# An attention-then-feed-forward kernel on one core: float32 loads for three head pairs, fills written ahead of loads, another order of loads, and a head pair moved behind the first feed-forward units

## The chip, the cores and the metric

The kernel runs on 1 core of one Trainium2 chip. The metric is the device time of one execution in microseconds; lower is better. Runs of one kernel agree within 1%, mostly within 0.5%. The profile is of one execution; its span (first to last instruction) is about 2 us shorter than the timed figure.

## The reference

```python
# attention: B, H, S, D = 8, 8, 576, 64, float32
scores = q @ k^T / 8 + bias[bucket(|i - j|)]      # T5 bias: a 32-entry table for each head
attn = softmax(scores);  x = attn @ v              # -> x: (B*S, H*D) = (4608, 512)
# bilinear feed-forward
a = x @ w_a;  b = x @ w_b                          # 512 -> 1536
out = (a * b) @ w_out                              # 1536 -> 512
```

## The kernel before

The heads are taken in pairs: 8 batches of 4 pairs, 32 in all, so pair 4 is the first of batch 1. 576 positions are 512 ("main") and 64 ("tail"). A pair takes scores on TensorE, the exponential on ScalarE, a multiply by the exponential of the bias on VectorE (only near the diagonal), and the product with V on TensorE. A column of ones beside V makes the sum of the softmax. The feed-forward work is cut into units (`ff_a`, `ff_b`, `ff_o`), which are put between the steps of the pairs from stage 4 on, so that TensorE is never without work. Stage s means the steps issued around pair s.

All loads before the first stage, in the order of the program (float32 to bf16 is cast on the way in GpSimd's queue):

```python
for p in range(2):                                    # pairs 0 and 1 in float32
    for h in range(2):
        load_h(nc.sync, q, q32[:, p, :, h, :], 0, 2 * p + h)
        load_h(nc.scalar, k, k32[:, p, :, h, :], 0, 2 * p + h)
# ... fills, bias table computed ...
nc.sync.dma_start(out=tab.ap(), in_=tab_sb[0:H, :])   # the table goes to HBM
load_w(nc.sync, 0)                                    # and comes back as W, one band for each pair
# ... Wt, the band of the tails, two transfers ...
load_w(nc.sync, 1)

load_tails(0)                    # GpSimd's queue from here on: tails of batches 0 and 1
load_t(q, qn, 0, 4, 8)           # pairs 2 and 3
load_t(k, kn, 0, 4, 8)
load_v(0)
load_pad(v, vt, 0)               # V's tails of batches 0 and 1
load_t(q, qn, 1, 0, 8)           # batch 1
load_t(k, kn, 1, 0, 8)
load_w_in(0)
load_w_in(1)
load_v(1)                        # V of batch 1, into vm[1]
load_w_in(2)
```

The first four pairs run without units. Stage 0 ends so:

```python
for s in range(4):
    ex(s, 0)
    if s > 0:
        mul(s - 1, 3)                                 # last bias multiply of the pair before
        mul_tail(s - 1)
    # ... transposes of the next pair, scores, exponentials, product with V ...
    mul(s, 2)
    # ...
    if s == 0:
        for i in range(2):
            nc.vector.memset(att_sb[i][:, 1088:1152], 0.0)
        nc.vector.memset(vm[1][:, :, :, Dh:Dh + 1], 1.0)      # ones beside V, second buffer
```

Stage 4 (pair 4) has its scores ahead of the first unit `U`; the number of units of each stage is in `quotas`:

```python
quotas = {4: 5, 5: 7, 6: 7, 7: 7, 8: 7}               # 9 from stage 9 on
steps += [mul(3, 3), mul_tail(3), t_x(2, FF), c_x(2),
          t_q(4, TR), c_q(4, ACT), t_k(4, FF), c_k(4),
          A(0, 1, 2), N(0), qk1(4, 0), ex(4, 0), A(3, 4), N(3),
          qk1(4, 1), ex(4, 1), t_x(3, TR), c_x(3),
          t_q(5, FF), qk1(4, 2), ex(4, 2), c_q(5),
          qk1(4, 3), ex(4, 3), U, mul(4, 0), ...]     # lambdas left out here
```

The program order is kept on every engine. The framework adds a semaphore wait wherever an instruction touches a buffer that an earlier one in the program writes.

The softmax here doesn't subtract the row's maximum and nothing guards it: scores larger than these inputs give would overflow.

## Time and profile before

| | before |
|---|---|
| time, median of 4 (3 were known for the prediction: 452.51) | 452.88 us (452.20 to 453.74) |
| span of the profiled run | 450.3 us |
| TensorE busy | 414.0 us (92%) |
| VectorE, longest wait | 25.6 us, once |

In all views PE is TensorE (PEld its weight loads), DVE VectorE, ACT ScalarE, POOL GpSimd and SP SyncE; L328 is line 328 of the kernel. The page first: busy time of the engines, then tenths of TensorE's busy time, of its granted clock and of the 16 DMA engines in 40 equal slices of 11.26 us.

```profile
span 450.3 us, 8335 instructions
...
PE 414.0 (92%) x3350; PEld 204.5 (45%) x3350; DVE 196.7 (44%) x488; ACT 241.8 (54%) x340; POOL 112.3 (25%) x142
...
PE   7311899999999999999999999999999999999995
...
PEclk9755999999999999999999999999999999999999
DMA  9999999969990999099909990941021002002004
```

The 92% is an average of two kernels: slices 2 to 4 hold little TensorE work (three tenths to one tenth), nearly all others are full. The same in figures, by the windows view (packets overlap, so its DMA share can pass 1):

```profile
core 0: us, PE busy (x) PEld busy (x) DVE busy (x) ACT busy (x) POOL busy (x), PEclk, DMA share, GB/s
11.00:22.00 11.00, 4.41 (x31) 2.02 (x29) 2.47 (x9) 6.43 (x8) 10.19 (x13) 0.72 1.80 159
22.00:33.00 11.00, 2.13 (x23) 1.65 (x24) 0.00 (x0) 0.00 (x0) 8.69 (x11) 0.50 3.25 141
33.00:44.00 11.00, 0.76 (x13) 0.76 (x13) 1.89 (x9) 0.46 (x2) 7.25 (x10) 0.50 1.75 183
...
112.00:450.00 338.00, 333.78 (x2551) 159.52 (x2548) 143.03 (x330) 184.70 (x265) 44.75 (x54) 1.00 0.72 77
```

Between 22 and 33 us neither VectorE nor ScalarE runs anything. The list of waits of the first 90 us (engine and line, what released it, us in all, times, longest) says who is to blame:

```profile
DVE at L328 <- DMA vm<-in_v_dram: 25.6, 1, 25.6
ACT att L347 <- PE qktt L340: 23.4, 2, 23.2
...
PE qktt L340 <- DVE QT L229: 15.6, 1, 15.6
...
PE av L370 <- DMA vt<-in_v_dram: 6.2, 1, 6.2
```

Linked together: ScalarE (L347) waits for TensorE (L340), TensorE for VectorE (L229), VectorE for the load of V. But line 328 is the bias multiply, and it reads no V. VectorE's timeline (start, us, then what ran, and in brackets the idle time before it) shows the real one:

```profile
15.93 0.55 DVE L328 TENSOR_TENSOR at<-at,W 128x768 bf16<-128x768 bf16 x1
16.43 0.13 DVE L566 MEMSET att<- 128x32 uint32 x2
42.11 0.45 DVE L328 TENSOR_TENSOR at<-at,W 128x512 bf16<-128x512 bf16 x1 [25.56 <-DMA vm<-in_v_dram]
42.23 0.09 DVE L567 MEMSET vm<- 128x32 bf16 x1
42.48 0.25 DVE L354 TENSOR_TENSOR att<-att,Wt 128x192 bf16<-128x192 bf16 x1
```

In the program the memset of line 567 stands directly after the two of line 566, ahead of the multiply. It writes the ones into `vm[1]`, and `load_v(1)`, which writes the same buffer, stands far above it in the program. So it waits for that load. The last part landed at 41.98 us; the record of the semaphore wait in VectorE's queue carries line 567 and stands at 42.01 us. The multiply's record begins at 42.11 us, ahead of the memset's at 42.23, though it stands behind it in the program; so the idle time was booked to the multiply.

### The profile page before, as it was taken

The page shows a single profiled execution, that of the slowest core. Times are in us where ns is not written, and L with a number is a line of the kernel's source. Part 1 is how long each engine was busy: PE and PEld are TensorE (multiplying, and loading weights), DVE is VectorE, ACT ScalarE, POOL GpSimd, SP SyncE. Part 2 cuts the span into 40 slices and gives each one's busy share as a digit, 9 for nine tenths or more (in the row PEclk, how much of TensorE's full clock was granted, in tenths as well). Part 3 has the DMA queues.
Part 4 walks back from the last instruction along what each step waited for, and adds up shares of the span by engine and source line. Part 5 has one row for each costly group of instructions (what it writes and reads, how often), then busy time and mean ns, then how long its engine had stood idle before and what let it go on. Part 6 is the DMA issues. An engine that isn't in the chain of part 4 may idle for free.

```text
span 450.3 us, 8335 instructions
## 1 busy us (share of the span) xinstructions
PE 414.0 (92%) x3350; PEld 204.5 (45%) x3350; DVE 196.7 (44%) x488; ACT 241.8 (54%) x340; POOL 112.3 (25%) x142
## 2 busy tenths in 40 slices
PE   7311899999999999999999999999999999999995
PEld 3111555455444444454445444544454454444442
DVE  5102867554455345534553455345534550330330
ACT  3501866565666566656665666566656642323321
POOL 8885750608300910092009100300000000000000
PEclk9755999999999999999999999999999999999999
DMA  9999999969990999099909990941021002002004
GB/s 148 156 148 184 182 155 166 92 40 130 166 108 13 112 185 110 13 109 192 117 13 115 185 104 15 143 120 38 13 84 38 15 13 96 0 1 93 0 1 93
DMA packets 173895, 41.74 MB, mean 93 GB/s; under 512 B 160408, under 2 KB 169248, under 8 KB 173856
## 3 DMA queue, kind: packets, MB, share of 16 engines
q0 software_dynamic: 116336, 18.36, 65.9%
q1 hardware_dynamic: 55264, 22.22, 27.8%
q10 hardware_dynamic: 2256, 0.62, 0.7%
q8 instruction: 26, 0.43, 0.4%
q14 instruction: 13, 0.11, 0.1%
HBM read 38.83 MB, written 9.45 MB: 107 GB/s over the span
## 4 chain that ended last, share of the span: by engine, by line
PE 88%; DMA 5%; POOL 3%; DVE 1%; ACT 1%; issue 1%; DVEq 0%; ACTq 0%; POOLq 0%
PE pb L444 22%; PE pa L434 21%; PE po L454 21%; PE av L379 9%; PE qk L309 7%; DMA vm<-in_v_dram 4%; PE av L370 2%; PE qkt L334 2%; DMA kn<-in_k_dram 2%; PE qkt L337 1%; POOL vm L131 1%; POOL kn L122 1%; POOL qn L122 1%; PE trx L412 1%; DVE XG L388 1%
## 5 line engine op out<-in xcount | busy, mean ns | idle before, releaser
L320 ACT ACTIVATE at<-qk 128x1024 bf16<-128x1024 f32 x128 | 126.3, 1024 | 29.3 <-PE qk L309 28.8
L447 DVE TENSOR_TENSOR g<-pb,ha 128x512 bf16<-128x512 f32 x108 | 74.7, 691 | 123.7 <-PE pb L444 104.9
L434 PE MATMUL pa<-xn,wa 128*128 128x512 bf16 x432 | 111.0, 379 | 0.0
L444 PE MATMUL pb<-xn,wb 128*128 128x512 bf16 x432 | 110.9, 379 | 0.0
L438 ACT ACTIVATE ha<-pa 128x512 f32<-128x512 f32 x108 | 64.6, 598 | 70.8 <-PE pa L434 70.7
L454 PE MATMUL po<-wo,g 128*128 128x512 bf16 x432 | 102.5, 379 | 0.0
L328 DVE TENSOR_TENSOR at<-at,W 128x512 bf16<-128x512 bf16 (+1 forms) x128 | 60.4, 483 | 39.0 <-DMA vm<-in_v_dram 25.6
L444 PEld LDWEIGHTS <-wb 128*128 128x128 bf16 x432 | 38.7, 97 | 52.5 <-issue 17.2
L434 PEld LDWEIGHTS <-wa 128*128 128x128 bf16 x432 | 38.9, 98 | 50.4 <-issue 11.0
L131 POOL DMA_DIRECT2D vm<-in_v_dram x32 | 28.2, 909 | 126.3 <-PE av L379 125.0
L454 PEld LDWEIGHTS <-g 128*128 128x128 bf16 x432 | 38.4, 98 | 45.9 <-issue 7.6
L458 ACT ACTIVATE ob<-po 128x512 f32<-128x512 f32 x36 | 21.5, 597 | 68.3 <-PE po L454 68.3
L379 PE MATMUL av<-vm,at 128*128 128x65 bf16 x1024 | 48.1, 196 | 0.0
L379 PEld LDWEIGHTS <-at 128*128 128x128 bf16 x1024 | 43.4, 99 | 6.6
L370 PE MATMUL av<-vt,att 128*128 128x130 bf16 x160 | 35.5, 222 | 6.2 <-DMA vt<-in_v_dram 6.2
L387 DVE RECIPROCAL rc<-av 128x6 f32<-128x6 f32 x64 | 12.0, 188 | 54.2 <-PE av L379 54.2
L348 ACT ACTIVATE att<-qkt 128x1024 bf16<-128x1024 f32 x32 | 32.7, 1022 | 0.0
L122 POOL DMA_DIRECT2D qn<-in_q_dram x32 | 27.9, 911 | 17.9 <-PE trq L263 17.6
L388 DVE TENSOR_TENSOR XG<-av,rc 128x384 bf16<-128x384 f32 x64 | 31.4, 491 | 2.2
L122 POOL DMA_DIRECT2D kn<-in_k_dram x32 | 27.9, 910 | 8.4 <-DMA vt<-in_v_dram 5.1
L309 PE MATMUL qk<-QTb,KTb 64*128 64x512 bf16 x192 | 29.1, 381 | 0.0
L347 ACT ACTIVATE att<-qktt 128x64 bf16<-128x64 f32 x32 | 7.2, 225 | 29.0 <-PE qktt L340 28.8
(96 smaller groups left out, 211.8 us busy)
## 6 DMA issues: line engine op xcount, KB each, us to landing
out_dram<-ob SPq DMA_DIRECT2D x32, 256.0 KB, 3.5
vm<-in_v_dram POOLq DMA_DIRECT2D x32, 128.0 KB, 6.1
qn<-in_q_dram POOLq DMA_DIRECT2D x28, 128.0 KB, 9.2
kn<-in_k_dram POOLq DMA_DIRECT2D x28, 128.0 KB, 11.8
wa<-in_moe_w_a_dram POOLq DMA_DIRECT2D x6, 256.0 KB, 8.5
wb<-in_moe_w_b_dram POOLq DMA_DIRECT2D x6, 256.0 KB, 8.5
wo<-in_moe_w_out_dram POOLq DMA_DIRECT2D x1, 1536.0 KB, 16.9
out_dram<-ob SPq DMA_DIRECT2D x8, 128.0 KB, 2.3
```

Of the source, the lines that this page charges most:

```text
L122: nc.gpsimd.dma_start(out=dst[b % 2][:, :].rearrange("p (t h d) -> p t h d", h=H, t=NM)[:, t, h0:h1, :], in_=src[b, h0:h1, 128 * t:128 * t ...
L309: nc.tensor.matmul(out=ps[:, hh, :], lhsT=kT_(p, t)[r, :], rhs=qT[r, :, :], start=True, stop=True)
L320: nc.scalar.activation(out=at[:, :, :], in_=ps[:, :, :], func=ACTF.Exp, scale=scale)
L328: nc.vector.tensor_tensor(out=at[:, :, lo:hi], in0=at[:, :, lo:hi], in1=w[:, :, y:(None if z < 0 else z):-1], op=MULT)
L370: nc.tensor.matmul(out=pav[:, slot, :, :], lhsT=x, rhs=vt[b // 2 % 2][:, 4 * i + hp, :, :], start=True, stop=True)
L379: nc.tensor.matmul(out=pav[:, slot, hh, :], lhsT=x, rhs=vm[i][:, 2 * hp + hh, t, :], start=False, stop=True, skip_group_check=True)
L388: nc.vector.tensor_tensor(out=xg[:, j0:j0 + n, :, :], in0=pav[:, 0:n, :, 0:Dh], in1=rc.unsqueeze(3).to_broadcast([128, n, 2, Dh]), op=MULT)
L434: nc.tensor.matmul(out=pa[:, :], lhsT=wa_sb[df // FW][:, mc, 128 * (df % FW):128 * (df % FW) + 128], rhs=xn_sb[mc][:, xin(c)], start=(mc = ...
L438: nc.scalar.activation(out=ha[:, :], in_=pa[:, :], func=ACTF.Copy)
L444: nc.tensor.matmul(out=pb[:, :], lhsT=wb_sb[df // FW][:, mc, 128 * (df % FW):128 * (df % FW) + 128], rhs=xn_sb[mc][:, xin(c)], start=(mc = ...
L447: nc.vector.tensor_tensor(out=g_sb[df][:, :], in0=pb[:, :], in1=ff["ha"][:, :], op=MULT)
L454: nc.tensor.matmul(out=po[:, :], lhsT=g_sb[df][:, 128 * tt:128 * tt + 128], rhs=wo_sb[:, df, :], start=(df == 0), stop=(df == NDF - 1))
```

## The change

Its intent: give the first head pairs everything they need sooner. Pair 2 and the tails of batch 0 come in float32 by SyncE's queue, V of pair 0 comes first in GpSimd's, the first feed-forward weights come ahead of batch 1, the ones and zeros are written before the loads into their buffers, and pair 4 is put behind the first units. The core of the diff (left out: helpers, renamings, the float32 transposes of pair 2 and of the tails, and fills of later batches that move from VectorE to GpSimd or to a later place):

```diff
-    for p in range(2):
-        for h in range(2):
-            load_h(nc.sync, q, q32[:, p, :, h, :], 0, 2 * p + h)
-            load_h(nc.scalar, k, k32[:, p, :, h, :], 0, 2 * p + h)
+    load32(0, q, q32, (nc.sync, nc.sync))
+    load32(0, k, k32, (nc.scalar, nc.scalar))
+    load32(1, q, q32, (nc.sync, nc.sync))
+    load32(1, k, k32, (nc.sync, nc.sync))
...
+    load_pad(nc.sync, k, kt32, 0, 1)            # tails of batch 0 in float32
+    load_pad(nc.sync, q, qt32, 0, 1)
...
+    for i in range(2):
+        nc.vector.memset(vm[i][:, :, :, Dh:Dh + 1], 1.0)     # both, before any load
+        nc.vector.memset(att_sb[i][:, 1088:1152], 0.0)
...
     nc.sync.dma_start(out=tab.ap(), in_=tab_sb[0:H, :])
+    load32(2, q, q32, (nc.sync, nc.sync))       # pair 2
+    load32(2, k, k32, (nc.sync, nc.sync))
     load_w(nc.sync, 0)
...
-    load_tails(0)
-    load_t(q, qn, 0, 4, 8)
-    load_t(k, kn, 0, 4, 8)
-    load_v(0)
-    load_pad(v, vt, 0)
+    load_vp(0, 0)
+    load_vt(0, 1)
+    load_p(q, qn, 0, 3)
+    load_p(k, kn, 0, 3)
+    load_vp(0, 1)
+    load_t(v, None, 0, 4, 8)
+    load_w_in(0)
+    for x in (ktl, qtl):
+        pad(nc.gpsimd, x[0][:, 4:8, :, :], Dh)
+    load_tails(1, 1)
     load_t(q, qn, 1, 0, 8)
     load_t(k, kn, 1, 0, 8)
-    load_w_in(0)
     load_w_in(1)
+    pad(nc.gpsimd, vt[0][:, 4:8, :, :], Dh + 1)
+    ones(nc.gpsimd, vt[0][:, 4:8, :, :])
+    load_vt(1, 1)
     load_v(1)
...
-        if s == 0:
-            for i in range(2):
-                nc.vector.memset(att_sb[i][:, 1088:1152], 0.0)
-            nc.vector.memset(vm[1][:, :, :, Dh:Dh + 1], 1.0)
...
-    quotas = {4: 5, 5: 7, 6: 7, 7: 7, 8: 7}
+    quotas = {4: 7, 5: 7, 6: 7, 7: 6, 8: 6}
...                                              # stage 4; "lambda:" left out
-  mul(3, 3), mul_tail(3), t_x(2, FF), c_x(2), t_q(4, TR), c_q(4, ACT), t_k(4, FF), c_k(4),
-  A(0, 1, 2), N(0), qk1(4, 0), ex(4, 0), A(3, 4), N(3), qk1(4, 1), ex(4, 1), t_x(3, TR), c_x(3),
-  t_q(5, FF), qk1(4, 2), ex(4, 2), c_q(5), qk1(4, 3), ex(4, 3), U, mul(4, 0), ...
+  mul(3, 3), mul_tail(3), t_x(2, FF), c_x(2), A(0, 1, 2), N(0), A(3, 4), N(3), t_x(3, FF), c_x(3), U,
+  t_q(4, TR), c_q(4, ACT), U, t_k(4, TR), c_k(4), U, qk1(4, 0), ex(4, 0), qk1(4, 1), ex(4, 1), U,
+  qk1(4, 2), ex(4, 2), mul(4, 0), qk1(4, 3), ex(4, 3), mul(4, 1), U, ...
```

More of the change, by code (lines that the diff above doesn't have):

```diff
@@ L90 @@
     id32 = const.tile([128, 128], FP32, name="id32")
-    q32 = const.tile([128, 2, NM, 2, Dh], FP32, name="q32")
-    k32 = const.tile([128, 2, NM, 2, Dh], FP32, name="k32")
+    q32 = const.tile([128, 3, NM, 2, Dh], FP32, name="q32")
+    k32 = const.tile([128, 3, NM, 2, Dh], FP32, name="k32")
+    qt32 = const.tile([128, H // 2, 2, Dh], FP32, name="qt32")
+    kt32 = const.tile([128, H // 2, 2, Dh], FP32, name="kt32")
     qn = [wpool.tile([128, H * NM * Dh], BF16, name=f"qn{i}") for i in range(2)]
@@ L122, in load_t @@
             nc.gpsimd.dma_start(
-                out=dst[b % 2][:, :].rearrange("p (t h d) -> p t h d", h=H, t=NM)[:, t, h0:h1, :],
+                out=(vm[b % 2][:, h0:h1, t, 0:Dh] if dst is None else
+                     dst[b % 2][:, :].rearrange("p (t h d) -> p t h d", h=H, t=NM)[:, t, h0:h1, :]),
                 in_=src[b, h0:h1, 128 * t:128 * t + 128, :].transpose([1, 0, 2]))
@@ L129, in load_v, with load_p, load_vp, load_pad @@
     def load_v(b):
-        for t in range(NM):
-            nc.gpsimd.dma_start(
-                out=vm[b % 2][:, :, t, 0:Dh],
-                in_=v[b, :, 128 * t:128 * t + 128, :].transpose([1, 0, 2]))
-    def load_pad(src, dst, b):
-        for hh in range(2):
-            nc.gpsimd.dma_start(
-                out=dst[b // 2 % 2][64 * hh:64 * hh + 64, :, hh, 0:Dh],
-                in_=src[b:b + 2, hh:H:2, SM:S, :].rearrange("b h c d -> c (b h) d"))
-    def load_tails(b):
-        load_pad(k, ktl, b)
-        load_pad(q, qtl, b)
+        load_t(v, None, b, 0, 8)
+    def load_p(src, dst, b, hp):
+        x = dst[b % 2][:, :].rearrange("p (t h d) -> p t h d", h=H, t=NM)
+        for h in (2 * hp, 2 * hp + 1):
+            load_h(nc.gpsimd, src, x[:, :, h, :], b, h)
+    def load_vp(b, hp):
+        for h in (2 * hp, 2 * hp + 1):
+            load_h(nc.gpsimd, v, vm[b % 2][:, h, :, 0:Dh], b, h)
+    def load_pad(eng, src, dst, b, nb):
+        for hh in range(2):
+            eng.dma_start(
+                out=dst[64 * hh:64 * hh + 64, 4 * (b % 2):4 * (b % 2) + 4 * nb, hh, 0:Dh],
+                in_=src[b:b + nb, hh:H:2, SM:S, :].rearrange("b h c d -> c (b h) d"))
+    def load_tails(b, nb):
+        load_pad(nc.gpsimd, k, ktl[b // 2 % 2], b, nb)
+        load_pad(nc.gpsimd, q, qtl[b // 2 % 2], b, nb)
+    def load_vt(b, nb):
+        load_pad(nc.gpsimd, v, vt[b // 2 % 2], b, nb)
     def load_w_in(part):
@@ L162, with pad, ones, load32 @@
                                     ap=[[0, NB], [1, H]]))
-    for p in range(2):
-        for h in range(2):
-            load_h(nc.sync, q, q32[:, p, :, h, :], 0, 2 * p + h)
-            load_h(nc.scalar, k, k32[:, p, :, h, :], 0, 2 * p + h)
-    def pad(eng, x, i, n):
-        eng.memset(x[i][0:64, :, 1, 0:n], 0.0)
-        eng.memset(x[i][64:128, :, 0, 0:n], 0.0)
-    def ones(i):
-        nc.vector.memset(vt[i][0:64, :, 0, Dh:Dh + 1], 1.0)
-        nc.vector.memset(vt[i][64:128, :, 1, Dh:Dh + 1], 1.0)
-        nc.vector.memset(vm[i][:, :, :, Dh:Dh + 1], 1.0)
+    def pad(eng, x, n):
+        eng.memset(x[0:64, :, 1, 0:n], 0.0)
+        eng.memset(x[64:128, :, 0, 0:n], 0.0)
+    def ones(eng, x):
+        eng.memset(x[0:64, :, 0, Dh:Dh + 1], 1.0)
+        eng.memset(x[64:128, :, 1, Dh:Dh + 1], 1.0)
+    def load32(p, src, out, engs):
+        for h in range(2):
+            load_h(engs[h], src, out[:, p, :, h, :], 0, 2 * p + h)
+    load32(0, q, q32, (nc.sync, nc.sync))
+    load32(0, k, k32, (nc.scalar, nc.scalar))
+    load32(1, q, q32, (nc.sync, nc.sync))
+    load32(1, k, k32, (nc.sync, nc.sync))
     nc.vector.memset(zero_sb[:, :], 0.0)
-    for x in (ktl, qtl):
-        pad(nc.gpsimd, x, 1, Dh)
-        pad(nc.vector, x, 0, Dh)
+    pad(nc.vector, kt32, Dh)
+    pad(nc.vector, qt32, Dh)
+    load_pad(nc.sync, k, kt32, 0, 1)
+    load_pad(nc.sync, q, qt32, 0, 1)
     nc.vector.memset(tab_sb[0:H, 0:127], 1.0)
@@ L183 @@
     nc.vector.tensor_copy(out=id32[:, :], in_=ident)
-    pad(nc.vector, vt, 0, Dh + 1)
+    pad(nc.gpsimd, vt[0][:, 0:4, :, :], Dh + 1)
+    ones(nc.gpsimd, vt[0][:, 0:4, :, :])
+    for i in range(2):
+        nc.vector.memset(vm[i][:, :, :, Dh:Dh + 1], 1.0)
+        nc.vector.memset(att_sb[i][:, 1088:1152], 0.0)
     nc.vector.tensor_tensor(out=bt_sb[0:NB, :], in0=bt_sb[0:NB, :], in1=bl_sb[0:NB, :],
                             op=mybir.AluOpType.subtract)
-    ones(0)
     warm = ps_ff.tile([128, 512], FP32, tag="ffn", name="warm")
@@ L283, in t_k @@
             nc.tensor.transpose(ps[:, 128 * t:128 * t + 128], blocks(kn, p)[:, t, :, :], ident)
-        t_tails(p, ps, SM)
+        if p > 3:
+            t_tails(p, ps, SM)
         st[p]["k"] = ps
@@ L289, in c_k @@
             return
-        copy(eng, KT[p % 2][:, :], st[p]["k"][:, 0:SM + 256])
+        n = SM + 256 if p > 3 else SM
+        copy(eng, KT[p % 2][:, 0:n], st[p]["k"][:, 0:n])
     def turn(b, what):
@@ L499, with q_next, k_next, tails_next @@
     qk1(0, 1)
-    def two32(src, where, out):
-        ps = bank(where, FP32, "tr1")
-        for t in range(NM):
-            t32(ps, src, 1, t)
-        copy(None, out, ps[:, :])
-    def tails01():
-        ps = bank(FF, BF16, "trt01")
-        for p in range(2):
-            t_tails(p, ps, 256 * p)
-            copy(None, KT[p][:, SM:SM + 256], ps[:, 256 * p:256 * p + 256])
+    def q_next(s):
+        if s < 2:
+            ps = bank(TR, FP32, f"trq{s + 1}")
+            for t in range(NM):
+                t32(ps, q32, s + 1, t)
+            copy(None, QT[(s + 1) % 2][:, :], ps[:, :])
+        elif s == 2:
+            t_q(3, TR)
+            c_q(3)
+    def k_next(s):
+        if s < 2:
+            ps = bank(FF, FP32, f"trk{s + 1}")
+            for t in range(NM):
+                t32(ps, k32, s + 1, t)
+            copy(None, KT[(s + 1) % 2][:, 0:SM], ps[:, :])
+        elif s == 2:
+            t_k(3, FF)
+            c_k(3)
+    def tails_next(p0, n, eng):
+        if p0 + n > 4:
+            return
+        ps = bank(FF, FP32, f"trt{p0}")
+        for i in range(2 * n):
+            nc.tensor.transpose(ps[:, 128 * i:128 * i + 128],
+                                (qt32 if i % 2 else kt32)[:, p0 + i // 2, :, :], id32[:, :])
+        for i in range(n):
+            copy(eng, KT[(p0 + i) % 2][:, SM:SM + 256], ps[:, 256 * i:256 * i + 256])
     def gate(hp):
@@ L521 @@
             mul_tail(s - 1)
-        if s in (1, 2):
-            t_q(s + 1, TR)
-            c_q(s + 1)
-        if s == 0:
-            two32(q32, TR, QT[1][:, :])
+        q_next(s)
         if s > 1:
@@ L532 @@
             c_x(s - 2)
-        if s in (1, 2):
-            t_k(s + 1, FF)
-            c_k(s + 1)
-        if s == 0:
-            two32(k32, FF, KT[1][:, 0:SM])
+        k_next(s)
         qk1(s, 3)
@@ L540 @@
         if s == 0:
-            tails01()
+            tails_next(0, 2, None)
+        else:
+            tails_next(s + 1, 1, None)
         if s > 0:
@@ L563 @@
             qk1(s + 1, 1)
-        if s == 0:
-            for i in range(2):
-                nc.vector.memset(att_sb[i][:, 1088:1152], 0.0)
-            nc.vector.memset(vm[1][:, :, :, Dh:Dh + 1], 1.0)
         if s == 2:
@@ L573 @@
             load_t(k, kn, 2, 0, 8)
-            load_tails(2)
+            for x in (ktl, qtl):
+                pad(nc.gpsimd, x[1], Dh)
+            load_tails(2, 2)
             load_w_out()
@@ L580, in load_qkt @@
         if b % 2 == 0:
-            load_tails(b)
+            load_tails(b, 2)
     def turns(s):
@@ L598 @@
             steps += [lambda: mul(3, 3), lambda: mul_tail(3), lambda: t_x(2, FF), lambda: c_x(2),
-                      lambda: t_q(4, TR), lambda: c_q(4, ACT), lambda: t_k(4, FF), lambda: c_k(4),
-                      A(0, 1, 2), N(0), lambda: qk1(4, 0), lambda: ex(4, 0), A(3, 4), N(3),
-                      lambda: qk1(4, 1), lambda: ex(4, 1), lambda: t_x(3, TR), lambda: c_x(3),
-                      lambda: t_q(5, FF), lambda: qk1(4, 2), lambda: ex(4, 2), lambda: c_q(5),
-                      lambda: qk1(4, 3), lambda: ex(4, 3), U, lambda: mul(4, 0),
-                      lambda: qk_tail(4), lambda: ex_tail(4), U, lambda: mul(4, 1), U,
-                      lambda: t_k(5, TR), lambda: c_k(5), lambda: mul(4, 2),
-                      U, lambda: mul(4, 3), lambda: mul_tail(4), U]
+                      A(0, 1, 2), N(0), A(3, 4), N(3), lambda: t_x(3, FF), lambda: c_x(3), U,
+                      lambda: t_q(4, TR), lambda: c_q(4, ACT), U, lambda: t_k(4, TR), lambda: c_k(4), U,
+                      lambda: qk1(4, 0), lambda: ex(4, 0), lambda: qk1(4, 1), lambda: ex(4, 1), U,
+                      lambda: qk1(4, 2), lambda: ex(4, 2), lambda: mul(4, 0),
+                      lambda: qk1(4, 3), lambda: ex(4, 3), lambda: mul(4, 1), U,
+                      lambda: qk_tail(4), lambda: ex_tail(4), lambda: mul(4, 2),
+                      lambda: t_q(5, TR), lambda: c_q(5), U, lambda: mul(4, 3),
+                      lambda: t_k(5, TR), lambda: c_k(5), lambda: mul_tail(4), U]
         elif new:
@@ L638 @@
         if s == 4:
-            pad(nc.vector, vt, 1, Dh + 1)
-            nc.vector.memset(vt[1][0:64, :, 0, Dh:Dh + 1], 1.0)
-            nc.vector.memset(vt[1][64:128, :, 1, Dh:Dh + 1], 1.0)
+            pad(nc.gpsimd, vt[1], Dh + 1)
+            ones(nc.gpsimd, vt[1])
+            for x in (ktl, qtl):
+                pad(nc.gpsimd, x[0][:, 0:4, :, :], Dh)
         if new and s % 4 == 2 and b + 1 < B:
@@ L647 @@
                 if b % 2 == 0:
-                    load_pad(v, vt, b)
+                    load_vt(b, 2)
     put_units(len(units) - nxt)
```

## The prediction

> **What bounds the kernel now.** By the page's busy totals TensorE is busy 414.0 of 450.3 us. By the windows view, from 112 us to the end it is busy 333.8 of 338 us: nothing to win there. The loss lies before 44 us, where it is busy 15.9 of 44 us and its clock is granted at 0.50 from 22 to 44 us. (The Trainium skill, "TensorE: Matmul & The Clock Gate", Part 1: idle halves the clock. The trace agrees: it is 1.00 again from 56 us.) The list of waits names one cause: VectorE waits 25.6 us, once, for the load of V of batch 1. The timeline shows it: VectorE stops at 16.5 us and goes on at 42.1 us, 0.03 us after that load's last landing (41.98). What waits there isn't the bias multiply of pair 0 that the list names, but the instruction ahead of it in the program, the memset of ones in the second V buffer, written after the loads into that buffer. The multiply needs only W, landed at 15.0. All else (the first queries' tail, 23.2 us of ScalarE; 15.6 us of TensorE; the fourth W) hangs on it.
>
> **What the change does.** It writes those ones before the loads, so this wait goes. Putting V and its tail of pair 0 first in GpSimd's queue removes TensorE's next wait (6.2 us, V tail landed 25.5). It adds no TensorE work that counts (float32 transposes for pair 2: under 1 us). It moves no fewer bytes: pair 2's q and k have as many rows in float32 as before.
>
> **What takes its place.** The bias table goes through SyncE's queue, now behind 2,048 more rows ahead of the table's store and, for W, 2,048 rows of pair 2. The Trainium skill, "DMA: Bandwidth & Descriptors", "Queues, rings and completion order": engines take turns between queues packet by packet; so with GpSimd's queue full SyncE gets about half of the roughly 1,000 packets/us that the DMA table shows (9,946 in 20–30 us). My estimate: table landed at 13 instead of 10.4 us, first W at 18 instead of 15.0, tail W at 20 instead of 17.1. So VectorE passes the multiply of pair 0 at about 20 instead of 42.1 us: 22 us won.
>
> **Does the rest follow?** From there the pairs repeat the old rhythm: fifth pair's stage at 33 (was 55.3), its first unit at 36 (was 61.0). DMA is saturated until 85 us and doesn't get faster, so slack is consumed. Estimated landings against needs: q and k of batch 1 at 32 and 36 (needed 36 and 38); second weights 38 (40); V of batch 1 42 (47); output weights 74.5 as before (needed about 75 instead of 96.7); keys of batch 2, transposed, 76–77 (needed at 77.5; pair 8 began at 98.8). The last two are tight: 0 to 3 us may come back as waits. Reordering pair 4 saves about 0.5 us of bubbles; moving units between stages moves no total.
>
> **Prediction: 430 us**, 8 in 10 within 424 to 439. Chances: faster by over 2% 0.96, within 2% 0.03, slower 0.01.
>
> **What would show it.** Right: VectorE's 25.6 us wait gone; a wait of VectorE for W of 3 to 6 us ending near 18–20; fifth stage's first feed-forward matmul at 34–38 us; TensorE's total idle from 36 us to about 14; from 112 us nothing changed. Wrong: if first W lands by 15 us the queue estimate failed (gain 25 us); if it lands after 22, gain 18.
>
> **What would make it wrong.** TensorE waiting for output weights or batch 2's transposed keys between 70 and 80 us (then 432–440); another write-after-write wait hidden behind the removed one; SyncE's queue stalling longer; V of batch 0 late behind float32 loads.

## The result, and the profile after

| | before | after |
|---|---|---|
| time, median of 4 | 452.88 us | 433.87 us (433.51 to 434.36) |
| ratio | | 0.958, 95% interval 0.9559 to 0.9601 |
| span of the profiled run | 450.3 us | 432.3 us |

A ratio here is the mean time of one kernel's runs over that of the other's of the same rounds, so it isn't quite the ratio of the medians quoted. The change is 4.2% faster.

The page after (same lines as before; a slice is now 10.8 us):

```profile
span 432.3 us, 8313 instructions
...
PE 411.5 (95%) x3296; PEld 204.4 (47%) x3350; DVE 195.9 (45%) x482; ACT 241.4 (56%) x340; POOL 118.1 (27%) x164
...
PE   6688898999999999999999999999999999999995
...
PEclk9599999999999999999999999999999999999999
DMA  9999999999909990999099908931021002002004
```

The hole in slices 2 to 4 is gone, and the DMA engines are as full as before. 54 records of matmuls are missing here (3,296 of 3,350; the weight loads are all there), so TensorE's idle time can't be read as a difference of busy times; below I use weight loads to tell when a piece of work began. The windows view after:

```profile
11.00:22.00 11.00, 7.66 (x38) 4.17 (x39) 2.93 (x10) 5.55 (x7) 9.80 (x16) 0.54 1.77 193
22.00:33.00 11.00, 9.51 (x148) 6.43 (x149) 10.38 (x33) 8.92 (x13) 9.59 (x15) 1.00 2.09 180
33.00:44.00 11.00, 9.33 (x128) 5.86 (x127) 5.89 (x20) 4.65 (x8) 10.01 (x14) 1.00 1.73 164
...
112.00:432.00 320.00, 313.60 (x2369) 150.88 (x2405) 133.83 (x308) 172.54 (x248) 40.56 (x48) 1.00 0.67 73
```

The list of waits of the first 90 us after:

```profile
ACT ha L468 <- PE pa L464: 13.6, 9, 4.9
...
DVE at L358 <- DMA W<-bias_tab: 4.2, 1, 4.2
```

And VectorE's timeline at the place of the old wait:

```profile
19.37 0.90 DVE L358 TENSOR_TENSOR at<-at,W 128x512 bf16<-128x512 bf16 x2 [4.19 <-DMA W<-bias_tab]
...
20.20 0.89 DVE L358 TENSOR_TENSOR at<-at,W 128x768 bf16<-128x768 bf16 x2
21.54 0.26 DVE L384 TENSOR_TENSOR att<-att,Wt 128x192 bf16<-128x192 bf16 x1 [0.45 <-DMA Wt<-bias_tab]
21.71 0.22 DVE L387 TENSOR_TENSOR att<-att,W 128x128 bf16<-128x128 bf16 x1
```

The 25.6 us wait is now one of 4.2 us for W (landed at 19.28) and one of 0.45 us for the tail's W (21.41). The tail's multiply runs at 21.54 us where it ran at 42.48: 20.9 us won at this place. But only 18.0 us are left at the end. Where the rest went is seen from the start of the scores of each pair (first weight load of each, from the traces):

| scores of pair | before, us | after, us | difference |
|---|---|---|---|
| 2 | 44.53 | 23.58 | 20.95 |
| 3 | 49.96 | 29.63 | 20.33 |
| 5 | 66.42 | 50.20 | 16.22, with 2 units more done |
| 9 | 103.61 | 85.65 | 17.96, the same work done |
| 31 | 345.32 | 327.36 | 17.96 |
| span | 450.30 | 432.34 | 17.96 |

From pair 9 on the difference no longer moves. Some 2.4 us were lost between pair 3 and pair 9, where stage 4 lies. ScalarE's timeline of that stage after:

```profile
33.92 1.03 ACT L378 ACTIVATE att<-qkt 128x1024 bf16<-128x1024 f32 x1
39.85 0.60 ACT L468 ACTIVATE ha<-pa 128x512 f32<-128x512 f32 x1 [4.90 <-PE pa L464]
40.34 0.59 ACT L255 ACTIVATE QT<-trq 128x512 bf16<-128x512 bf16 x1
42.38 0.60 ACT L468 ACTIVATE ha<-pa 128x512 f32<-128x512 f32 x1 [1.45 <-PE pa L464]
42.88 3.77 ACT L350 ACTIVATE at<-qk 128x1024 bf16<-128x1024 f32 x4
46.49 0.64 ACT L468 ACTIVATE ha<-pa 128x512 f32<-128x512 f32 x1
46.97 0.28 ACT L377 ACTIVATE att<-qktt 128x64 bf16<-128x64 f32 x1
47.07 1.09 ACT L378 ACTIVATE att<-qkt 128x1024 bf16<-128x1024 f32 x1
```

ScalarE has nothing to do for 4.9 us while pair 3 ends and the first unit begins, then four exponentials, copies of units and the tail's exponentials stand in line from 42.4 to 48.2 us. This suggested the first three theories to be tested: A, that the memset alone made the 25.6 us wait; C, that the new order of stage 4 costs about 2 us; E, that W comes late because it waits in SyncE's queue.

### The profile page after: what moved, and what is told of

It is laid out like the page before. It is cut to its first block, busy times and chain, and to the rows that moved or that the text cites. A ratio compares the mean times of both kernels' runs of the same rounds, so it can differ in the third digit from the quotient of the medians.

```text
span 432.3 us, 8313 instructions
## 1 busy us (share of the span) xinstructions
PE 411.5 (95%) x3296; PEld 204.4 (47%) x3350; DVE 195.9 (45%) x482; ACT 241.4 (56%) x340; POOL 118.1 (27%) x164
## 4 chain that ended last, share of the span: by engine, by line
PE 90%; DVE 3%; DMA 2%; ACT 2%; issue 1%; SPq 0%; ACTq 0%; DVEq 0%
PE pb L474 23%; PE po L484 22%; PE pa L464 21%; PE av L409 9%; PE qk L339 7%; PE av L400 2%; PE qkt L364 2%; PE qkt L367 1%; DMA qt<-in_q_dram 1%; DMA k<-in_k_dram 1%; DVE XG L418 1%; ACT at L350 1%; DVE at L358 1%; DVE g L477 1%; PE qktt L370 0%
## 5 line engine op out<-in xcount | busy, mean ns | idle before, releaser
L464 PE MATMUL pa<-xn,wa 128*128 128x512 bf16 x415 | 109.8, 379 | 0.8
L474 PE MATMUL pb<-xn,wb 128*128 128x512 bf16 x414 | 109.4, 379 | 1.0 <-DVE g L477 0.2
L484 PE MATMUL po<-wo,g 128*128 128x512 bf16 x416 | 99.6, 379 | 1.0 <-issue 0.2
L464 PEld LDWEIGHTS <-wa 128*128 128x128 bf16 x432 | 38.8, 98 | 49.3 <-issue 10.3
L124 POOL DMA_DIRECT2D qn<-in_q_dram x28 | 24.8, 914 | 12.9 <-PE qk L339 5.8
L124 POOL DMA_DIRECT2D kn<-in_k_dram x28 | 24.7, 900 | 13.0 <-DMA vt<-in_v_dram 4.6
L400 PEld LDWEIGHTS <-att 128*128 128x128 bf16 x160 | 15.8, 99 | 7.3 <-issue 0.7
```

Of the source, the lines that this page charges most:

```text
L124: nc.gpsimd.dma_start(out=(vm[b % 2][:, h0:h1, t, 0:Dh] if dst is None else dst[b % 2][:, :].rearrange("p (t h d) -> p t h d", h=H, t=NM)[ ...
L400: nc.tensor.matmul(out=pav[:, slot, :, :], lhsT=x, rhs=vt[b // 2 % 2][:, 4 * i + hp, :, :], start=True, stop=True)
L464: nc.tensor.matmul(out=pa[:, :], lhsT=wa_sb[df // FW][:, mc, 128 * (df % FW):128 * (df % FW) + 128], rhs=xn_sb[mc][:, xin(c)], start=(mc = ...
L474: nc.tensor.matmul(out=pb[:, :], lhsT=wb_sb[df // FW][:, mc, 128 * (df % FW):128 * (df % FW) + 128], rhs=xn_sb[mc][:, xin(c)], start=(mc = ...
L484: nc.tensor.matmul(out=po[:, :], lhsT=g_sb[df][:, 128 * tt:128 * tt + 128], rhs=wo_sb[:, df, :], start=(df == 0), stop=(df == NDF - 1))
```

## The experiments

Twelve kernels were run, all correct. "Kernel before" in each group's rounds had a median of 451.55 us (first group), 452.35 (second) and 452.62 (third).

### The memset alone

```diff
-            nc.vector.memset(vm[1][:, :, :, Dh:Dh + 1], 1.0)      # end of stage 0
...
     ones(0)
+    nc.vector.memset(vm[1][:, :, :, Dh:Dh + 1], 1.0)
```

> The kernel before with one statement moved: the ones of the second V buffer are written before the loads into it. Theory A (VectorE waited 25.6 us for that buffer's loads only because this memset stands behind them): the wait goes, the next one is TensorE's for the tail of V of batch 0, landed at 25.5 us; the chain goes on about 15.7 us earlier, 436.6 us (434.5 to 439). Rival B (the multiply itself waited, for W or for the order of the loads): no change, 452 to 454 us. If A holds, this one line is worth most of the 19 us, and all the rest of the change about 3 us.

Measured: 436.25 us (434.99 to 436.47), ratio 0.9647 (0.961 to 0.9683). The span is 434.66 us, and every pair from 3 on begins 15.65 us earlier than before. The longest DMA wait of TensorE in the first 90 us is now the one named:

```profile
PE av L371 <- DMA vt<-in_v_dram: 6.7, 1, 6.7
```

Theory A is shown for this direction: one line moved wins 15.64 us of span, and the next wait, for V's tail, takes over.

### The memset put back in the changed kernel

```diff
-        nc.vector.memset(vm[i][:, :, :, Dh:Dh + 1], 1.0)          # for both i
+    nc.vector.memset(vm[0][:, :, :, Dh:Dh + 1], 1.0)
...
+        if s == 0:
+            nc.vector.memset(vm[1][:, :, :, Dh:Dh + 1], 1.0)      # end of stage 0
```

> The changed kernel with that one statement put back behind the loads. Theory A: VectorE stands still from about 21 us until V of batch 1 has landed (40.96 us in the changed kernel), the stage of the fifth pair begins near 54 instead of 35 us, 451 to 454 us: the whole gain gone. Rival B (the float32 loads, the order of loads and the moved pair give the gain together): only part is lost, 436 to 446 us.

Measured: 452.77 us (452.34 to 453.85), ratio 1.0022 (0.9984 to 1.0059). The list of waits shows the old wait again, shorter only because VectorE comes to it later:

```profile
DVE at L358 <- DMA vm<-in_v_dram: 19.8, 1, 19.8
```

All else of the change is worth nothing as long as this wait stands: pair 3 begins only 0.61 us earlier than before, and the new stage 4 then takes 2.39 us. That is theory A from the other side.

### Stage 4 in its old order

The list of steps of stage 4 and `quotas` of the kernel before, in the changed kernel:

```diff
-    quotas = {4: 7, 5: 7, 6: 7, 7: 6, 8: 6}
+    quotas = {4: 5, 5: 7, 6: 7, 7: 7, 8: 7}
...
-  ... A(3, 4), N(3), t_x(3, FF), c_x(3), U, t_q(4, TR), c_q(4, ACT), U, ..., U, qk1(4, 0), ex(4, 0), ...
+  ... t_q(4, TR), c_q(4, ACT), t_k(4, FF), c_k(4), A(0, 1, 2), N(0), qk1(4, 0), ex(4, 0), A(3, 4), ...
```

> The changed kernel with the fifth pair's stage and the unit quotas as before. Theory C (the gain shrinks from 20.3 us at the entry of that stage to 18.0 us at its exit because pair 4 was moved behind the first units: ScalarE is idle 4.9 us, then its exponentials and copies come in a bunch and TensorE waits): gain stays near 20, 431.8 us (430.8 to 432.8). Rival D (what is lost there is DMA: q and k of batch 1, landed at 30.9 and 33.9 us, or weights): pair 4 in front then waits for its data and the time stays at 433.5 or goes up.

Measured: 431.48 us (431.02 to 431.93), ratio 0.9547 (0.9513 to 0.9581). Each pair from 3 to 31 begins 20.63 us earlier than before: nothing is lost in stage 4. ScalarE's timeline there:

```profile
33.62 1.04 ACT L378 ACTIVATE att<-qkt 128x1024 bf16<-128x1024 f32 x1
36.22 0.60 ACT L255 ACTIVATE QT<-trq 128x512 bf16<-128x512 bf16 x1 [1.56 <-PE trq L291]
37.83 2.08 ACT L350 ACTIVATE at<-qk 128x1024 bf16<-128x1024 f32 x2 [1.01 <-PE qk L339]
40.30 1.94 ACT L350 ACTIVATE at<-qk 128x1024 bf16<-128x1024 f32 x2 [0.39 <-DVE xn L257]
42.12 0.61 ACT L468 ACTIVATE ha<-pa 128x512 f32<-128x512 f32 x1
```

The exponentials of pair 4 now fill the time in which pair 3 ends, and no load is late: the scores of pair 4 begin at 37.39 instead of 42.27 us. The spans differ by 432.34 - 429.67 = 2.67 us, of which 0.30 us lies before pair 3 (20.63 against 20.33), where both have the same program. The intervals of the two ratios overlap, so the traces decide: between pair 3 and pair 9 the changed kernel loses 2.37 us, and the two other kernels with its stage 4 and quotas (the memset put back; the keys of pair 1 on ScalarE's queue, below) 2.39 and 2.38 us; with the old stage 4 the lead moves by 0.01 us at most, here and in five other experiments with a fast profile (the one exception, pair 2 in bf16, waits for a load). Rival D falls, and of theory C it is shown that the order costs this. That the cost comes by way of ScalarE is read from the two timelines, not tested alone.

### The new order with the old quotas

```diff
-    quotas = {4: 7, 5: 7, 6: 7, 7: 6, 8: 6}
+    quotas = {4: 5, 5: 7, 6: 7, 7: 7, 8: 7}
```

> The changed kernel with the new order of the fifth stage but the old numbers of units in stages 5 to 9 (5, 7, 7, 7, 7 for 7, 7, 7, 6, 6). Theory C1 (the order, pair 4 behind the first units, costs the 2 us): 433.9 us within 0.5. Rival C2 (too many units in that stage cost them): 431.5 to 432.3 us.

Measured: 434.30 us (434.19 to 435.44), ratio 0.9594 (0.9578 to 0.961). So it is the order: the old number of units doesn't bring the loss back. This kernel has the same units in each stage as the one before, and its lead over that falls from 21.22 us at pair 3 to 16.62 us at pair 5, by 4.60 us. The windows view of 33 to 51 us, for the changed kernel, the one with the old stage 4 and this one:

```profile
33.00:51.00 18.00, 14.71 (x164) 8.34 (x164) 10.12 (x29) 9.78 (x15) 14.64 (x19) 1.00 1.68 175
33.00:51.00 18.00, 15.91 (x207) 9.99 (x205) 11.64 (x34) 11.38 (x16) 14.53 (x18) 1.00 1.75 180
33.00:51.00 18.00, 13.76 (x139) 7.83 (x138) 9.50 (x27) 8.90 (x14) 14.30 (x18) 0.91 1.77 179
```

Here TensorE was busy least, and its granted clock was 0.5 from 44.46 to 47.87 us, while it stayed at 1.00 in the other two. The profiled run is also the slowest of this kernel's four, by 1.0 us. So the 4.60 us are not the order's cost alone, and how much of it two units more fill isn't settled; the medians, of different rounds, differ by 0.4 us.

### The keys of pair 1 on ScalarE's queue

```diff
-    load32(1, k, k32, (nc.sync, nc.sync))
+    load32(1, k, k32, (nc.scalar, nc.scalar))
```

> The changed kernel with the keys of pair 1 on ScalarE's queue again, as before: 1,024 rows fewer ahead of tails and bias table in SyncE's queue. Theory E (W at 19.3 and tail W at 21.4 us came late because they stand behind those rows in one queue): tails and table about 1 us earlier, W near 18.3, 0.5 to 1 us less: 433.0 us. Rival F (the DMA engines are full, so which queue carries the rows doesn't matter): W again at 19 to 19.5, time within 0.3 us of 433.9.

Measured: 433.43 us (432.51 to 433.90), ratio 0.9587 (0.9545 to 0.963). W landed at 18.55 us. That is between what the theories expected, and it can't be told from chance: the changed kernel, the one with the old stage 4 and the one with the old quotas have the same program up to pair 3, and there pair 2 begins at 23.58, 23.29 and 22.70 us; here at 23.00. So I tried it together with the old stage 4.

> The changed kernel with the old order of the fifth pair's stage (alone 431.5 us) and keys of pair 1 on ScalarE's queue (alone 433.4 us) together. If the two causes lie one after the other on the same chain, the gains add: about 0.7 us below the first of them, 430.8 us (430.2 to 431.4). If not, 431.5.

Measured: 431.19 us (430.33 to 432.13), ratio 0.9533 (0.9506 to 0.956). W landed at 19.38 us in this run, later than the 18.90 without the edit. Inconclusive: no gain of this edit is shown.

### V first in GpSimd's queue, without the float32 path for pair 2

The kernel before with the memset moved, and:

```diff
-    load_t(q, qn, 0, 4, 8)
-    load_t(k, kn, 0, 4, 8)
     load_v(0)
     load_pad(v, vt, 0)
+    load_t(q, qn, 0, 4, 8)
+    load_t(k, kn, 0, 4, 8)
```

> The kernel before with the ones early (as in the first experiment, 436.25 us) and, in GpSimd's queue, V of batch 0 with its tail ahead of the bf16 q and k of pairs 2 and 3. Theory A2 (one queue carries all of it, and all of it is due at once: what is put first only makes the other late, so V first pays only together with pair 2 on another queue): V's tail lands near 19 to 20 instead of 25.6 us, but k of pair 2 near 25 instead of 18; TensorE now waits for that k, and the time stays within 1.5 us of the first experiment: 435 to 438 us. Rival G (V's lateness was the cause, the order alone cures it): 433 us or less.

Measured: 434.88 us (434.83 to 437.64), ratio 0.9629 (0.9594 to 0.9665). V's tail landed at 19.18 us, the last k of pairs 2 and 3 at 24.09 instead of 18.2 us. TensorE's list of waits has the same time under another name:

```profile
PE trq L264 <- DMA qn<-in_q_dram: 6.3, 4, 5.5
```

The median is 1.4 us better than with V in its old place, just under the 435 to 438 expected, but with one run of four at 437.64 and intervals that overlap a gain isn't settled by the times. In the traces the lead from pair 3 on is 17.24 instead of 15.65 us. A2 holds in the main: what is put first makes the other late.

### The table first in SyncE's queue

Old stage 4, keys of pair 1 on ScalarE's queue, and in SyncE's queue the bias table ahead of the tails and pair 2 behind the W of the tails:

```diff
-    load_pad(nc.sync, k, kt32, 0, 1)            # from ahead of the table ...
-    load_pad(nc.sync, q, qt32, 0, 1)
     nc.sync.dma_start(out=tab.ap(), in_=tab_sb[0:H, :])
-    load32(2, q, q32, (nc.sync, nc.sync))
-    load32(2, k, k32, (nc.sync, nc.sync))
+    load_pad(nc.sync, k, kt32, 0, 1)            # ... to behind it
+    load_pad(nc.sync, q, qt32, 0, 1)
     load_w(nc.sync, 0)
     # Wt
+    load32(2, q, q32, (nc.sync, nc.sync))
+    load32(2, k, k32, (nc.sync, nc.sync))
     load_w(nc.sync, 1)
```

> The last one, with SyncE's queue in another order: bias table, tails of batch 0, W of pair 0, tail W, then pair 2's float32 q and k, then W of pair 1. Theory E (W waits in line in its own queue): first W lands at 13.5 to 15 us instead of 18.6, tail W near 16; pair 2's k becomes the late one (19 to 20 us); pair 2 begins 1 to 2 us earlier than 23.0 us, 429.6 us (428.8 to 430.6). Rival F (the 16 engines are full and only turns between queues count): W at 18 or later, time as in the last one.

Measured: 436.35 us (436.28 to 437.18), ratio 0.9651 (0.9628 to 0.9674). My figure was wrong by 7 us. W did land earlier, at 15.38 us, about as theory E says, but q and k of pair 2 landed at 20.04 and 23.91 us, not 19 to 20, and TensorE waited for them:

```profile
PE trq L515 <- DMA q<-in_q_dram: 3.4, 1, 3.4
PE trk L515 <- DMA k<-in_k_dram: 2.2, 1, 2.2
```

Pair 2 began at 29.02 instead of 23.49 us. The place that the change had given pair 2, in the gap between the table's store and its return, was better than this one: SyncE waits there anyway.

### GpSimd's fills ahead of its loads

```diff
     ones(nc.gpsimd, vt[0][:, 0:4, :, :])
+    for x in (ktl, qtl):
+        pad(nc.gpsimd, x[0][:, 4:8, :, :], Dh)
+    pad(nc.gpsimd, vt[0][:, 4:8, :, :], Dh + 1)
+    ones(nc.gpsimd, vt[0][:, 4:8, :, :])
...                                              # and the same six lines taken out further down
```

On top of the last kernel:

> The same again with all of GpSimd's zero and one fills for batch 0's and 1's tails ahead of its first load, so that its queue begins some 2 to 3 us later and leaves SyncE's queue the engines until about 6 us. Theory H (GpSimd's early loads of V, not due before 17 us, take half of the engines from what is due first): tails of batch 0 land 1 us earlier, all W too, 0.5 to 1.5 us gained: 428.8 us. Otherwise 429.6, or worse by up to 1 us if V of pair 0 gets late.

Measured: 434.02 us (432.75 to 434.36), ratio 0.9587 (0.9556 to 0.9618), 2.3 us better than the same without it, where 0.5 to 1.5 was expected; the figure of 428.8 stood on the wrong 429.6 for the kernel before this edit. GpSimd's first V load was issued at 5.26 instead of 3.62 us; the last tail landed at 12.37 instead of 13.06, W at 14.76 instead of 15.38, pair 2's last k at 21.31 instead of 23.91 us. Theory H holds here: loads that aren't due yet took engine time from those that are.

On top of the changed kernel with the old stage 4:

> The changed kernel with the old fifth stage (431.5 us), and GpSimd's fills for both batches' tails ahead of its first load, so that its queue starts 1.7 us later. Theory H (its early V loads take turns from SyncE's queue): tails of batch 0 near 11.7 instead of 12.4, W near 18.2 instead of 18.9 us, 430.6 us (429.8 to 431.2). If only the order in SyncE's own queue counts: 431.5.

Measured: 429.11, 429.40 and 431.34 us in the three timed rounds, ratio 0.9499 (0.9472 to 0.9527). This is the best of all kernels run, but its interval overlaps that of the kernel without the fills moved (0.9513 to 0.9581), so the gain of some 2 us over 431.48 is likely and not settled. The profiled execution took 1,052.63 us and gives no reading (see the end).

### Pair 2 in bf16 by GpSimd's queue

Old stage 4, and the float32 path for pair 2 undone:

```diff
-    load32(2, q, q32, (nc.sync, nc.sync))
-    load32(2, k, k32, (nc.sync, nc.sync))
...
     load_vt(0, 1)
+    load_p(q, qn, 0, 2)
+    load_p(k, kn, 0, 2)
     load_p(q, qn, 0, 3)
```

> The same kernel (431.5 us) with pair 2 undone: its q and k in bf16 by GpSimd's queue right behind V of pair 0, no float32 rows of it in SyncE's queue. Theory E2 (W stands in line behind pair 2's 2,048 rows): W lands near 16 to 17 instead of 18.9, tail W near 18.5 instead of 21.1, pair 2's k near 14.5; 430 us (429 to 431). If the float32 path of pair 2 is what the gain rests on: 433 us or more, TensorE waiting for pair 2.

Measured: 431.69 us (431.05 to 432.07), ratio 0.9536 (0.9522 to 0.9551): no difference from 431.48. W landed at 17.09 and the last tail W at 19.30 us, as E2 says, and pair 3 began 22.41 us earlier than before, 1.8 us more than with float32. But k of batch 1, now behind pair 2 in GpSimd's queue, landed at 35.42 instead of 33.50 us, TensorE's transposes of it waited for it twice between 34.3 and 35.5 us, and TensorE's granted clock was 0.5 from 36.09 to 39.50 us (1.00 there with the old stage 4 alone). The lead had fallen to 20.95 us at pair 4 and 20.26 us at pair 5. The gain was won in one place and given back in the next. The float32 path of pair 2 is therefore not what the gain rests on.

With the fills first as well:

> Pair 2 in bf16 by GpSimd and GpSimd's fills first, with the old fifth stage. If H and E2 both hold: W near 15.5 us and 429.2 us. The later start of GpSimd's queue can make pair 2's k late (16 us): then no better than the one of the two that is alone.

Measured: 433.90, 430.95 and 431.97 us in the timed rounds, ratio 0.955 (0.9518 to 0.9583): no better than pair 2 in bf16 alone. The profiled execution was slow again (2,319.48 us).

## Why the prediction was right, and where it was off

- **The cause: right.** The 25.6 us wait was the memset's. Moving it alone won 15.64 us; putting it back cost all.
- **The next bound: right in kind, a little short in size.** VectorE was to wait 3 to 6 us for W until 18 to 20 us: it waited 4.2 us until 19.3. My landings of 18 and 20 us for W and the tail's W were 19.28 and 21.41. So the term "22 us won" measured 20.9 us at the tail's multiply, and 20.6 us from pair 3 to the end in the kernel with the old stage 4.
- **The landings against needs: right.** q and k of batch 1 landed at 30.88 and 33.88 us, the second weights at 36.51, V of batch 1 at 40.96, the output weights at 72.75 and the turned keys of batch 2 at 74.71 us, all within 2.3 us of the estimates and all ahead of their need. The turned tails of these keys landed at 78.20 us, later than estimated for the keys but ahead of the first scores of pair 8 (80.11). The wait that I feared between 70 and 80 us didn't come.
- **The step that failed: "Reordering pair 4 saves about 0.5 us of bubbles".** It cost 2.4 us (2.67 by the spans). The step weighed TensorE's bubbles alone; in the new stage ScalarE was idle for 4.9 us and then had a queue. The first feed-forward matmul, which I put at 34 to 38 us, came at 38.8.
- **A test that I chose badly.** "TensorE's total idle from 36 us to about 14": 54 of its records are missing after, so the sum can't be had from the page.

The sum: predicted 22 + 0.5 us of span, measured 20.33 (at pair 3) - 2.37 = 17.96. Both terms were sized too high; the time, 433.87 us, is 3.9 us over the 430 predicted and lies in the range of 424 to 439.

The change is thus three things. The moved memset alone gives 15.64 us of span. The other loads and fills, with it, give 20.63 - 15.64 = 4.99 us more (4.8 by the medians of the same rounds), and without it 0.6 us at pair 3. These are single traces: three kernels with the same program up to there led by 20.33, 20.63 and 21.22 us at pair 3. The new stage 4 takes 2.4 us back.

The DMA engines are full from 2 to about 80 us, so the order of loads only decides who waits. The Trainium skill says this of queues in "DMA: Bandwidth & Descriptors", "Issuing engines are not separate DMA queues": transfers started by different engines "will ultimately run on the same 16 DMA engines and interleave with each other". The runs agree: V first (24.09 instead of 18.2 us for k), the table first (23.91 instead of 17.50 us for k of pair 2) and pair 2 in bf16 (35.42 instead of 33.50 us for k of batch 1) each mainly moved the wait. What did help was to start later what isn't due yet, and to use a gap in which a queue waits anyway.

What stays open: which of the other loads and fills win the 4.99 us (the float32 path of pair 2 doesn't, V first with the memset alone gave 1.6 us of span; the tails in float32 and the earlier first weights were not tried alone); whether the keys of pair 1 on ScalarE's queue help at all, and how much the fills ahead of GpSimd's loads are worth with the old stage 4, since its profile is lost.

## What to carry to other kernels

A fill of part of a buffer belongs ahead of the loads into that buffer in the program: behind them it waits for all of them, and in an engine that works in order everything behind it waits too. When the profile names an instruction that doesn't read what it is said to wait for, look at its neighbours in the program. When the transfers are the bound, ask of each load when it is due, and before moving work of one engine out of the way of another, look at what a third one will be doing in that time.

## What the Trainium skill lacked or had wrong

- "DMA: Bandwidth & Descriptors", "Bandwidth": it gives measured rates by the size of a transfer, and a packet's overhead in cycles, but no measured rate of this chip for full queues of short rows. With 256-byte rows read and 128 bytes written, the 16 engines moved 9,946 rows from 20 to 30 us before the change, about one row in a nanosecond, 133 GB/s as written, nearly all of them (9,844) by GpSimd's queue.
- The same page, "Queues, rings and completion order": that queues take turns packet by packet carried my estimate of W's landing (18 us, measured 19.28). I took half of about 1,000 rows in a us for SyncE's queue; from 5 to 19 us after the change it moved 5,502 of 12,547, which is 44% and 393 in a us. It doesn't say what that means for a load that is due: GpSimd's queue started 1.6 us later brought SyncE's last pair-2 load in 2.6 us sooner (21.31 for 23.91 us).
- "Perfetto Trace Analysis", "Sequencer Loop": it tells that an instruction waits for its semaphores in the engine's queue, but not that the wait can be shown at a neighbour. Here 25.6 us stood at the multiply of line 328, and the memset of line 567 was the one that waited.
- "TensorE: Matmul & The Clock Gate", Part 1, names a half and a full clock, one of 13/16 when three or more cores of a die work, and a warning of a clock stuck at a quarter for over 50 us. Two profiled executions here ran wholly at a lower rate: the 128x512 matmul of the units took 827 ns and 1,690 ns on average instead of 379, all other engines being normal (the multiply of VectorE in the units took 692 ns in both). Why isn't known: their traces hold no record of the granted clock, so the 1.0 that the results list for them is no measurement. The timed runs of the same kernels were fast. From the page of the slower one:

```profile
span 2317.7 us, 8315 instructions
...
L474 PE MATMUL pb<-xn,wb 128*128 128x512 bf16 x416 | 588.2, 1690 | 15.0 <-issue 15.0
```
